# Decoding 64-bit weights in a fused attention and feed-forward kernel: one merge for each part, and earlier second-weight loads

## The chip, the core and the metric

The kernel runs on one core of a Trainium2 chip. A core has five engines that run side by side and wait for each other by semaphores: TensorE (PE, matmuls), VectorE (DVE), ScalarE (ACT), GpSimd (POOL) and SyncE (SP, here only the issuer of DMAs). ScalarE issues some DMAs too. The metric is the device time of one execution in microseconds, from runs on the chip. A profile of one execution gives the rows that are quoted.

## The reference

Causal attention with a forget-gate bias, over 8 batches, 8 heads, 576 tokens and a head size of 64, and behind it a feed-forward block (FFN) from 512 to 2048 and back:

```python
scores = scale * np.matmul(q, k.transpose(0, 1, 3, 2))
s_pos = np.maximum(s, 0.0)
cum = np.cumsum(s_pos, axis=-1)
bias = -(cum[:, :, :, None] - cum[:, :, None, :])
scores = np.where(causal, -1000000000.0, scores + np.minimum(bias, 0.0))
attn = softmax(scores)                      # written out in the original
x = np.matmul(attn, v)                      # heads side by side: 4608 x 512
h = x @ w_in
g = np.where(h >= 1, h, np.where(h <= -1, 0.0, (h + 1) ** 2 / 4))
return (g @ w_out).astype(np.float32)
```

`w_in` (512 x 2048) and `w_out` (2048 x 512) come as 64-bit floats. The kernel gets them as pairs of 32-bit words, `lw` (low) and `hw` (high), and makes 32-bit floats of them on the chip.

## The kernel before

**Attention.** A job is two heads and one half of the query rows (`jobs`, 64 of them). `att_slot(j, k)` takes job `j` in eight slots: operands, six score units, output. A score unit is a matmul into PSUM (`s`, lines 434, 437 and 438), VectorE's reduction with the mask that writes `p` and the row minimum `mn` (line 443), ScalarE's exponential (454), then the scaling by `rs` and the transposes. The first four jobs (`plain`) scale with POOL and ScalarE (474, 472) and transpose on TensorE into `pp` (477, copied at 478); later ones split `p` into two 16-bit parts `pb` and transpose by DMA (508). `att_out` multiplies by `v` into `px`, and `x_split` writes `X`, the FFN's input, under the tag `x0` or `x1`, two buffers each.

**The FFN.** `ffn_h` makes `h` from `X` and `WI` (12 matmuls, line 596), ScalarE and VectorE make `u` (608, 611, 612), ScalarE and POOL split it into `g` (622, 623; tag `g`, four buffers). `ffn_y` multiplies `g` by `WO` (635).

**The weights.** Each weight comes in 16 parts of 128 x 512 numbers (512 KB). `Weights.load` (line 190) takes a raw buffer and issues the DMA on SyncE (line 200). The first weight's raw parts use the four `g` buffers, which the FFN takes over later. The second weight's use `raw`, `x0`, `raw` in turn, two buffers each; `X` of batch 0 also takes an `x0`. Its parts 0 to 2 have `after=w1.r[1]`: a one-column copy (line 195) into the raw buffer, which holds the DMA back until the second row block of the first weight has its scale.

`decode` (line 202) turns a raw part into 32-bit floats: ScalarE writes the absolute value of `hw` read as a float (208); VectorE clamps it from below and takes the peak of each row (209), shifts it by three bits and masks it (210), and puts in sign, exponent bit and the low bits. For even parts (`ACT_LOW`) ScalarE first writes the top bits of `lw` into `hw`'s lower half (215), and one merge follows (216). Odd parts take two merges, sign and exponent (218) and the low bits (219). From the peaks come power-of-two scales: `row_scale` and `row_shares` for the first weight, `scale` for each half of the second (groups of 8 parts), all of them through `exponent` (221). `split` makes two 16-bit parts of each number (257 to 265).

**The order.** The first weight's tasks (`w1_task`, decode part c, load part c + 3, split part c - 4) stand one in three slots among jobs 0 to 3, and the last of them behind these. `w2_tasks` gives the second weight's work: three loads, then for each group eight decodes (each with the load of part c + 3), the scale and eight splits. Six of these tasks come before the main loop, then two for each of its steps, with a higher priority. A planner with its own cost model puts all of it into a fixed order on each engine and each issue queue: it takes by priority whatever it reckons to be ready, so that an instruction without anything to wait for may come long before its place in the program. Each engine then works through its list in that order.

Of the kernel before, what the change touches and what calls it, by code (L numbers as in the profile page):

```python
# [7 lines left out]
BF16 = mybir.dt.bfloat16  # L8
F16 = mybir.dt.float16
F32 = mybir.dt.float32  # L10
F32R = mybir.dt.float32r
I32 = mybir.dt.int32
U16 = mybir.dt.uint16
U8 = mybir.dt.uint8
AF = mybir.ActivationFunctionType
ALU = mybir.AluOpType
# [6 lines left out]
P = 128  # L23
# [10 lines left out]
EPS = 1e-9  # L34
TINY = 2.0 ** -50
LEAST_A = 2.0 ** -5

LEAST_HI = 2.0 ** -15 * 1.125

UNITS = (  # L40
    [(i, hd, 0, QT[i][2]) for i in range(3) for hd in range(2)],
# [10 lines left out]
G_BUFS = 4  # L52
O_BUFS = 3
WO_LAG = 2
# [24 lines left out]
def attention_ffn(ctx: ExitStack, tc: tile.TileContext, qT, kT, vn, s, w_in, w_out, yT):  # L79
    nc = tc.nc  # L80
    LOADQ, CUMQ, FIRSTQ = nc.sync, nc.scalar, nc.sync
    V, A, G, T = nc.vector, nc.scalar, nc.gpsimd, nc.tensor

    cp = ctx.enter_context(tc.tile_pool(name="cp", bufs=1))
    ap = ctx.enter_context(tc.tile_pool(name="ap", bufs=2))
    gp = ctx.enter_context(tc.tile_pool(name="gp", bufs=2))
# [6 lines left out]
    floor_bias = cp.tile([P, 1], F32, name="floor_bias")  # L93
    V.memset(floor_bias, -31.0 / 64.0)

    def pow2floor(out, in_, least):
# [6 lines left out]
        out=ident, in_=ident, pattern=[[-1, P]], compare_op=ALU.not_equal,  # L103
# [13 lines left out]
    def spread(dst, top, name, bank=(ps_s, "s")):  # L117
# [10 lines left out]
        out=mask, in_=mask, pattern=[[-1, S]], compare_op=ALU.is_ge,  # L128
# [40 lines left out]
    NW = 16  # L169
    NC = 512  # L170
    WI = [cp.tile([P, 2, NC], F16, name=f"WI{c}") for c in range(NW)]
    WO = [cp.tile([P, 2, NC], F16, name=f"WO{c}") for c in range(NW + WO_LAG)]

    def flat32(t):
        return t.rearrange("p l n -> p (l n)").bitcast(F32)

    class Weights:
        def __init__(self, name, src, held, out, tags, groups, by_rows=False):
            self.size = NW // (NKT if by_rows else groups)
            self.name, self.src, self.held, self.out, self.tags = name, src, held, out, tags  # L180
            self.peak = cp.tile([P, NW], F32, name=f"peak_{name}")
            self.bound = [cp.tile([P, 1], F32, name=f"bound_{name}{g}") for g in range(groups)]
            self.r = [cp.tile([P, 1], F32, name=f"r_{name}{g}") for g in range(NW // self.size)]
            if by_rows:
                self.rows = cp.tile([P, NKT], F32, name=f"rows_{name}")
                self.shares = cp.tile([P, NKT], F32, name=f"shares_{name}")
            self.raw = {}
            self.act_low, self.pool_lo = ACT_LOW[name], POOL_LO[name]

        def load(self, c, after=None):  # L190
            if c < NW:
                pool, tag, bufs = self.tags[c % len(self.tags)]
                self.raw[c] = pool.tile([P, NC, 2], I32, tag=tag, bufs=bufs, name=f"{self.name}r{c}")
                if after is not None:
                    V.tensor_copy(self.raw[c][:, 0, :1], after.bitcast(I32))
                src = self.src(c)
                dst = self.raw[c]
                if len(src.shape) == 4:
                    dst = dst.rearrange("p (j n) t -> p j n t", j=2)
                nc.sync.dma_start(dst, src)  # L200

        def decode(self, c):
            raw = self.raw.pop(c)
            w = flat32(self.held[c])
            wi = w.bitcast(I32)
            lw, hw = raw[:, :, 0], raw[:, :, 1]

            A.activation(w, hw.bitcast(F32), AF.Abs)
            V.tensor_scalar(w, w, LEAST_HI, LEAST_HI, ALU.max, ALU.max, accum_out=self.peak[:, c:c + 1])
            V.tensor_scalar(wi, wi, 3, 0x3FFFFFF8, ALU.logical_shift_left, ALU.bitwise_and)  # L210

            if c in self.act_low:
                dst = raw.bitcast(U16).rearrange("p n (t f) -> p n t f", f=4)[:, :, 0, 2]
                src = raw.bitcast(U8).rearrange("p n (t f) -> p n t f", f=8)[:, :, 0, 3]
                A.activation(dst, src, AF.Identity, bias=floor_bias, scale=2.0 ** -5)
                V.scalar_tensor_tensor(wi, hw, -0x3FFFFFF9, wi, ALU.bitwise_and, ALU.bitwise_or)
            else:
                V.scalar_tensor_tensor(wi, hw, -0x40000000, wi, ALU.bitwise_and, ALU.bitwise_or)
                V.scalar_tensor_tensor(wi, lw, 29, wi, ALU.logical_shift_right, ALU.bitwise_or)

        def exponent(self, b):
            bi = b.bitcast(I32)
            V.tensor_scalar(bi, bi, 3, -0x40000000, ALU.logical_shift_left, ALU.bitwise_xor)
            V.tensor_scalar(bi, bi, 0x7F800000, None, ALU.bitwise_and)

        def scale(self, g, least):
# [39 lines left out]

    w1 = Weights(
        "wi", lambda c: w_in[c // 4 * P:(c // 4 + 1) * P, c % 4 * NC:(c % 4 + 1) * NC, :],
        WO, WI, ((gp, "g", G_BUFS),), 1, by_rows=True,
    )  # L270
    w2 = Weights(
        "wo", lambda c: w_out[c % 8 * 2 * P:(c % 8 + 1) * 2 * P, c // 8 * NC // 2:(c // 8 + 1) * NC // 2, :]
        .rearrange("(j p) n t -> p j n t", p=P),
        WO[WO_LAG:], WO, ((ap, "raw", 2), (gp, "x0", 2), (ap, "raw", 2)), 2,
    )
    a_in, b_out = w1.bound[0], w2.bound

# [51 lines left out]
    def batch_y(b, groups=(0, 1)):  # L329
        ysc.setdefault(b, {})  # L330
        for i in groups:
            y = ysc[b][i] = ap.tile([P, 1], F32, tag=f"ys{i}", name=f"ys{b}_{i}")
            V.tensor_scalar(y, gsc[b], b_out[i], 2.0 ** -28, ALU.mult, ALU.mult)
# [211 lines left out]
    held = {}  # L545
# [118 lines left out]
        w1.load(c)  # L664
    att_load(0, 0)
    def w2_tasks():
        for c in range(3):
            w2.load(c, w1.r[1])
        for g in range(2):
            for c in range(8 * g, 8 * g + 8):  # L670
                w2.decode(c)
                w2.load(c + 3)
                yield
            w2.scale(g, TINY)
            batch_y(0, (g,))
            for c in range(8 * g, 8 * g + 8):
                w2.split(c)
                yield

    def w1_task(c):  # L680
        w1.decode(c)
        w1.load(c + 3)
        if c >= NKT:
            w1.split(c - NKT)
        if c % NKT == NKT - 1:
            w1.row_scale(c // NKT, LEAST_A)

    c = 0
    for t in range(8 * NPAIR):
        if t % W1_SLOTS == 0:  # L690
            w1_task(c)
            c += 1
        if t == 2:
            load_v(0)
        if t == 6:
            batch_start(0)
        att_slot(t // 8, t % 8)
    for c in range(c, NW):
        w1_task(c)
# [10 lines left out]
    for n, hf in jobs[:NPAIR]:  # L710
        x_split(n, hf, held.pop((n, hf)), shares0)
    tasks = w2_tasks()
    for _ in range(W2_FIRST):
        next(tasks)

    t = 8 * NPAIR
# [56 lines left out]
```

## Time and profile before

| | us |
|---|---|
| median of 3 runs | 1091.19 |
| the runs | 1086.95, 1091.19, 1091.50 |
| the profiled execution | 1091.04 |
| its span, from the first to the last instruction | 1089.2 |

A row of the table of lines has: line, engine, operation, output and inputs, shapes, count; busy time in us and mean ns of one; idle time before them, and what ended it. A row of the answer for one line has the shortest, median and longest duration in ns. A row of a timeline has: start and duration in us, engine (SPq is SyncE's issuing of DMAs), line, operation. A row of waits has: who waited for whom, us in total, times, the longest. In the program's names `wir` and `wor` are the raw parts of the first and the second weight, and `WO` holds either weight's decoded numbers while they wait to be split.

### The profile page before, as it was taken

Reading aid. Unit: us, or ns where it says so; the run is one execution under the profiler, and the core shown is the slowest. Engines: PE = TensorE matmul, PEld = TensorE weight load, DVE = VectorE, ACT = ScalarE, POOL = GpSimd, SP = SyncE. Lnnn points to the kernel's source line nnn. Section 1 sums busy time; section 2 is a strip of 40 time slices with the busy share of each in tenths; the row PEclk is TensorE's granted clock in tenths of the full one; section 3 lists DMA queues with packets and bytes.
Section 4 is the critical chain, followed back from the end, with each engine's and each line's share of the span. In section 5 each row is a group of like instructions: output and inputs, shape, how many; then the busy total and the mean of one; then the engine's idle time right before and its main releaser. Section 6 shows DMA issues by size and latency. Waiting matters only on the chain.

```text
span 1089.2 us, 25029 instructions
## 1 busy us (share of the span) xinstructions
PE 1014.3 (93%) x8494; PEld 778.6 (71%) x8494; DVE 858.7 (79%) x2379; ACT 720.8 (66%) x1707; POOL 658.1 (60%) x1139
## 2 busy tenths in 40 slices
PE   3657889999999999999999999899999999999998
PEld 1334557787778877787778877787778877887787
DVE  7899977678788878887888888788888888887533
ACT  4776675567577675876577765776577765877432
POOL 4643677566577656666567665676577666665522
PEclk9999789999999999999999999999999999999999
DMA  8736543446357773777367753866376662676300
GB/s 248 232 105 191 151 85 82 113 106 160 89 133 151 141 153 74 165 140 163 78 157 140 156 124 88 157 147 157 70 171 142 140 138 69 152 131 140 69 25 20
DMA packets 300839, 140.33 MB, mean 129 GB/s; under 512 B 237608, under 2 KB 286632, under 8 KB 300712
## 3 DMA queue, kind: packets, MB, share of 16 engines
q1 hardware_dynamic: 291008, 128.80, 52.8%
q10 hardware_dynamic: 9704, 9.93, 3.2%
q8 instruction: 67, 1.10, 0.4%
q14 instruction: 60, 0.49, 0.1%
HBM read 71.00 MB, written 9.73 MB: 74 GB/s over the span
## 4 chain that ended last, share of the span: by engine, by line
PE 61%; DVE 10%; ACT 4%; issue 4%; POOL 3%; DMA 1%; ACTq 1%; DVEq 0%; POOLq 0%
PE h L596 26%; PE y L635 25%; PE px L537 4%; PE s L437 3%; PE s L438 3%; DVE pb L507 2%; DVE h L611 1%; DVE p L443 1%; DVE K2s L393 1%; ACT u L608 1%; DVE Q1s L392 1%; DVE u L612 1%; ACT p L454 1%; POOL pb L501 1%; POOL pb L504 1%
## 5 line engine op out<-in xcount | busy, mean ns | idle before, releaser
L596 PE MATMUL h<-x,WI 128*128 128x256 f16 (+1 forms) x3072 | 460.4, 290 | 7.4 <-DVE u L612 4.1
L635 PE MATMUL y<-g,WO 128*128 128x256 f16 (+1 forms) x3072 | 444.0, 286 | 2.0 <-ACT g L622 1.3
L596 PEld LDWEIGHTS <-WI 128*128 128x128 f16 x3072 | 287.8, 99 | 100.5 <-issue 17.7
L635 PEld LDWEIGHTS <-WO 128*128 128x128 f16 x3072 | 286.8, 98 | 83.5 <-issue 4.2
L623 POOL TENSOR_TENSOR g<-u,g 128x320 f16<-128x320 f32 (+1 forms) x256 | 207.3, 810 | 168.9 <-ACT g L622 160.8
L454 ACT ACTIVATE p<-p,mn 64x64 f32<-64x64 f32 (+4 forms) x320 | 179.4, 561 | 108.4 <-DVE mn L443 83.6
L608 ACT ACTIVATE u<-h,ub,us 128x320 f32<-128x320 f32 (+1 forms) x256 | 149.1, 583 | 130.1 <-PE h L596 128.5
L611 DVE SCALAR_TENSOR_TENSOR h<-h,ws,u 128x320 f32<-128x320 f32 (+1 forms) x256 | 132.7, 519 | 91.7 <-ACT u L608 88.5
L501 POOL TENSOR_SCALAR pb<-p,rs 128x256 f16<-128x256 f32 (+4 forms) x148 | 94.7, 640 | 138.6 <-DVE rs L497 86.3
L504 POOL TENSOR_TENSOR pb<-p,pb 128x256 f16<-128x256 f32 (+4 forms) x148 | 157.2, 1062 | 9.9
L443 DVE CUSTOM_DVE_ANT_0 p<-s,mask 64x64 f32<-64x64 f32 (+4 forms) x320 | 134.8, 422 | 29.8 <-PE s L438 19.9
L507 DVE SCALAR_TENSOR_TENSOR pb<-p,rs,pb 128x256 f16<-128x256 f32 (+4 forms) x148 | 128.8, 870 | 23.3 <-POOL pb L501 22.9
L612 DVE SCALAR_TENSOR_TENSOR u<-u,r,h 128x320 f32<-128x320 f32 (+1 forms) x256 | 130.5, 510 | 7.3
L437 PE MATMUL s<-K1s,Q1s 128*128 128x288 f32 (+4 forms) x312 | 118.0, 379 | 10.3 <-DVE mn L443 4.0
L502 ACT ACTIVATE p<-p,rs 128x192 f32<-128x192 f32 (+4 forms) x148 | 84.1, 568 | 48.8 <-DVE rs L497 47.1
L622 ACT CAST g<-u 128x320 f16<-128x320 f32 (+1 forms) x256 | 108.0, 422 | 7.7 <-DVE u L612 6.7
L503 POOL TENSOR_SCALAR pb<-p 128x256 f16<-128x256 f32 (+4 forms) x148 | 88.0, 595 | 21.0 <-ACT p L502 17.0
L438 PE MATMUL s<-K2s,Q2s 68*128 68x288 f32 (+4 forms) x312 | 96.1, 308 | 0.0
L537 PEld LDWEIGHTS <-vt 128*64 128x64 f16 x1464 | 67.5, 111 | 19.1 <-issue 13.6
L537 PE MATMUL px<-pt,vt 128*64 128x256 f16 (+3 forms) x1464 | 77.4, 255 | 1.4 <-DMA pt<-pb 1.3
L437 PEld LDWEIGHTS s<-K1s,Q1s 128*128 128x128 f32 (+1 forms) x312 | 56.5, 181 | 19.7 <-PE s L438 4.5
L393 DVE TENSOR_TENSOR K2s<-rk,K1s 64x1152 fp32r<-64x1152 f32 (+1 forms) x52 | 63.6, 1223 | 6.0 <-ACT K1s L390 4.7
(134 smaller groups left out, 1029.3 us busy)
## 6 DMA issues: line engine op xcount, KB each, us to landing
rk<-in_k_dram SPq DMA_DIRECT2D x56, 288.0 KB
wir<-in_moe_w_in_dram SPq DMA_DIRECT2D x16, 512.0 KB
v<-in_v_dram SPq DMA_DIRECT2D x32, 256.0 KB
wor<-in_moe_w_out_dram SPq DMA_DIRECT2D x16, 512.0 KB
rk<-in_k_dram SPq DMA_DIRECT2D x48, 160.0 KB
rq<-in_q_dram SPq DMA_DIRECT2D x48, 160.0 KB
rq<-in_q_dram SPq DMA_DIRECT2D x56, 128.0 KB
out_dram<-o ACTq DMA_DIRECT2D x32, 160.0 KB
```

The costliest lines, as they stand in the source:

```text
L437: T.matmul(sc[:R, :c1 - c0], Q1[:, hd, qo:qo + R], K1[:, hd, c0:c1], start=True, stop=False)
L443: ttr[0] = V.tensor_tensor_reduce(out=Pt[:R, c0:c1], in0=sc[:R, :c1 - c0], in1=mask[:R, mo:mo + c1 - c0], scale=-0.125, scalar=3.0e38 if m ...
L454: A.activation(Pt[:R, :W], Pt[:R, :W], AF.Exp, bias=m2[:R], scale=-1.0, accum_out=sums[n, i][:R, hd:hd + 1])
L504: G.tensor_tensor(los[1], pw, his[1], ALU.subtract)
L507: V.scalar_tensor_tensor(los[0], pv, rs[:R, :1], his[0], ALU.mult, ALU.subtract)
L537: T.matmul(px[hd * D:(hd + 1) * D, lo:N], vts[n][:, vl, j, hd * D:(hd + 1) * D], PT[:, 4 * j + 2 * hd + pl, lo:], start=(m == 0), stop=(m ...
L596: T.matmul(h[:, :N], WI[4 * kt + ft // 4][:, wl, ft % 4 * P:(ft % 4 + 1) * P], x[:, kt, xl], start=(n == 0), stop=(n == 3 * NKT - 1),)
L608: first = A.activation(u, h[:, :N], AF.Relu, bias=ubi[b], scale=usc[b]).ins
L611: V.scalar_tensor_tensor(h[:, :N], h[:, :N], wsc[b], u, ALU.mult, ALU.max)
L612: V.scalar_tensor_tensor(u, u, r, h[:, :N], ALU.min, ALU.mult)
L623: G.tensor_tensor(g[:, 1], u, g[:, 0], ALU.subtract)
L635: T.matmul(ys[b, hf, m][:, :N], WO[8 * (m // 2) + ft // 2][:, wl, c0:c0 + P], g[:, gl], start=(ft == 0 and n == 0), stop=(ft == NFT - 1 an ...
```

## The change

In `decode`, ScalarE's absolute value is scaled by 2^-112, which brings the exponent into range before the shift; the clamp and the mask go. VectorE shifts (one instruction), and a `tensor_tensor_reduce` adds the two halves of the row and takes the maximum of the sums as the peak. The low bits are put into `hw`'s lower half in both cases: by ScalarE for even parts, by a shift of 16-bit words on VectorE for odd ones. One merge then takes the sign and the low three bits from `hw`. `exponent` loses its shift and exclusive-or, as the peak is now taken from shifted numbers. The raw buffers of the second weight's parts 3 to 6 are the four `g` buffers. Parts 0 to 2 are loaded in the task of the first weight's part 12, with no copy to hold them back, parts 3 to 6 in the tasks of parts 12 to 15, part c + 7 behind the decodes of parts 0 to 2, and part c + 3 from part 7 on.

```diff
-LEAST_HI = 2.0 ** -15 * 1.125
...
+    sums2 = cp.tile([P, NC // 2], BF16, name="sums2")
...
             if c < NW:
-                pool, tag, bufs = self.tags[c % len(self.tags)]
+                pool, tag, bufs = self.tag(c)
...
-            lw, hw = raw[:, :, 0], raw[:, :, 1]
-
-            A.activation(w, hw.bitcast(F32), AF.Abs)
-            V.tensor_scalar(w, w, LEAST_HI, LEAST_HI, ALU.max, ALU.max, accum_out=self.peak[:, c:c + 1])
-            V.tensor_scalar(wi, wi, 3, 0x3FFFFFF8, ALU.logical_shift_left, ALU.bitwise_and)
-
+            hw = raw[:, :, 1]
+
+            A.activation(w, hw.bitcast(F32), AF.Abs, scale=2.0 ** -112)
+            V.tensor_scalar(wi, wi, 3, None, ALU.logical_shift_left)
+            half = w.shape[1] // 2
+            V.tensor_tensor_reduce(
+                out=sums2, in0=w[:, :half], in1=w[:, half:], scale=1.0, scalar=0.0,
+                op0=ALU.add, op1=ALU.max, accum_out=self.peak[:, c:c + 1],
+            )
+
+            low = raw.bitcast(U16).rearrange("p n (t f) -> p n t f", f=4)[:, :, 0, 2]
             if c in self.act_low:
-                dst = raw.bitcast(U16).rearrange("p n (t f) -> p n t f", f=4)[:, :, 0, 2]
                 src = raw.bitcast(U8).rearrange("p n (t f) -> p n t f", f=8)[:, :, 0, 3]
-                A.activation(dst, src, AF.Identity, bias=floor_bias, scale=2.0 ** -5)
-                V.scalar_tensor_tensor(wi, hw, -0x3FFFFFF9, wi, ALU.bitwise_and, ALU.bitwise_or)
+                A.activation(low, src, AF.Identity, bias=floor_bias, scale=2.0 ** -5)
             else:
-                V.scalar_tensor_tensor(wi, hw, -0x40000000, wi, ALU.bitwise_and, ALU.bitwise_or)
-                V.scalar_tensor_tensor(wi, lw, 29, wi, ALU.logical_shift_right, ALU.bitwise_or)
+                src = raw.bitcast(U16).rearrange("p n (t f) -> p n t f", f=4)[:, :, 0, 1]
+                V.tensor_scalar(low, src, 13, None, ALU.logical_shift_right)
+            V.scalar_tensor_tensor(wi, hw, -0x7FFFFFF9, wi, ALU.bitwise_and, ALU.bitwise_or)

         def exponent(self, b):
             bi = b.bitcast(I32)
-            V.tensor_scalar(bi, bi, 3, -0x40000000, ALU.logical_shift_left, ALU.bitwise_xor)
             V.tensor_scalar(bi, bi, 0x7F800000, None, ALU.bitwise_and)
...
-        WO[WO_LAG:], WO, ((ap, "raw", 2), (gp, "x0", 2), (ap, "raw", 2)), 2,
+        WO[WO_LAG:], WO,
+        lambda c: (gp, "g", G_BUFS) if 3 <= c < 7
+        else ((ap, "raw", 2), (gp, "x0", 2), (ap, "raw", 2))[(c if c < 3 else c + 2) % 3], 2,
...
     def w2_tasks():
-        for c in range(3):
-            w2.load(c, w1.r[1])
         for g in range(2):
             for c in range(8 * g, 8 * g + 8):
                 w2.decode(c)
-                w2.load(c + 3)
+                if c < 3:
+                    w2.load(c + 7)
+                elif c >= 7:
+                    w2.load(c + 3)
                 yield
...
     def w1_task(c):
         w1.decode(c)
         w1.load(c + 3)
+        if c == NW - 4:
+            for d in range(3):
+                w2.load(d)
+        if c >= NW - 4:
+            w2.load(c - NW + 7)
```

More of the change, by code (lines that the diff above doesn't have):

```diff
@@ L177, in attention_ffn, with __init__ @@
     class Weights:
-        def __init__(self, name, src, held, out, tags, groups, by_rows=False):
+        def __init__(self, name, src, held, out, tag, groups, by_rows=False):
             self.size = NW // (NKT if by_rows else groups)
-            self.name, self.src, self.held, self.out, self.tags = name, src, held, out, tags
+            self.name, self.src, self.held, self.out, self.tag = name, src, held, out, tag
             self.peak = cp.tile([P, NW], F32, name=f"peak_{name}")
@@ L268, in attention_ffn @@
         "wi", lambda c: w_in[c // 4 * P:(c // 4 + 1) * P, c % 4 * NC:(c % 4 + 1) * NC, :],
-        WO, WI, ((gp, "g", G_BUFS),), 1, by_rows=True,
+        WO, WI, lambda c: (gp, "g", G_BUFS), 1, by_rows=True,
     )
```

## The prediction

> **What bounds the kernel now.** I read the page first, then the windows by stage, then what TensorE waited for, then the decode's rows, then the timelines of SyncE and VectorE. The columns of a window are the busy time of PE, PEld, DVE, ACT and POOL (each with its instructions), the granted clock, the DMA share and GB/s.
>
> ```profile
> span 1089.2 us, 25029 instructions
> PE 1014.3 (93%) x8494; PEld 778.6 (71%) x8494; DVE 858.7 (79%) x2379; ACT 720.8 (66%) x1707; POOL 658.1 (60%) x1139
> ```
> ```profile
> 0.00:20.00 20.00, 3.31 (x10) 1.73 (x10) 14.49 (x37) 7.62 (x14) 7.30 (x22) 1.00 0.82 242
> 20.00:120.00 100.00, 66.98 (x215) 37.01 (x216) 91.21 (x277) 73.44 (x161) 53.26 (x80) 0.95 0.62 184
> 120.00:150.00 30.00, 26.23 (x171) 16.10 (x170) 24.35 (x69) 17.90 (x37) 16.46 (x20) 0.82 0.59 123
> 150.00:1089.20 939.20, 917.82 (x8103) 723.72 (x8101) 728.62 (x1999) 621.80 (x1498) 581.11 (x1018) 1.00 0.55 121
> ```
>
> TensorE is idle for 1089.2 - 1014.3 = 74.9 us. After 150 us it is busy 917.8 of 939.2: the matmuls set the time there, and nothing of the change lies there. Before 150 us it is idle 16.7 + 33.0 + 3.8 = 53.5 us. That start is where the weights are decoded, so the question is how much of those 53.5 us goes. From 20 to 120 us VectorE is busy 91.2 of 100 us, TensorE 67, and TensorE's longest waits are:
>
> ```profile
> PE s L434 <- DVE mn L443: 13.6, 9, 5.1
> PE pp L477 <- POOL p L474: 11.1, 4, 5.1
> PE col_wi L122 <- DVE t_wi L120: 3.1, 1, 3.1
> ```
>
> Two of the three end with VectorE, 16.7 us; the POOL step in between needs VectorE's `rs` as well. So in this stage **VectorE is the bound**, through an order fixed in advance, in which score reductions, weight decoding and scale chains queue behind one another.
>
> **The change, part by part: the decode.** Its groups in the table of lines, all on VectorE (busy us, mean ns):
>
> ```profile
> L209 DVE TENSOR_SCALAR_CACHE_REDUCE WO<-WO 128x512 f32<-128x512 f32 x32 | 21.6, 678 | 7.9 <-ACT WO L208 7.8
> L210 DVE TENSOR_SCALAR WO<-WO 128x512 int32<-128x512 int32 x32 | 17.2, 537 | 0.1
> L216 DVE SCALAR_TENSOR_TENSOR WO<-wir,WO 128x512 int32<-128x512 int32 x8 | 7.1, 884 | 0.0
> L218 DVE SCALAR_TENSOR_TENSOR WO<-wir,WO 128x512 int32<-128x512 int32 x8 | 6.4, 798 | 0.0
> L219 DVE SCALAR_TENSOR_TENSOR WO<-wir,WO 128x512 int32<-128x512 int32 x8 | 6.1, 766 | 0.0
> L218 DVE SCALAR_TENSOR_TENSOR WO<-wor,WO 128x512 int32<-128x512 int32 x8 | 6.1, 759 | 0.0
> L219 DVE SCALAR_TENSOR_TENSOR WO<-wor,WO 128x512 int32<-128x512 int32 x8 | 6.0, 754 | 0.0
> L216 DVE SCALAR_TENSOR_TENSOR WO<-wor,WO 128x512 int32<-128x512 int32 x8 | 5.9, 741 | 0.0
> L209 DVE DVE_READ_ACCUMULATOR WO<-WO 128x1 f32 x32 | 2.5, 79 | 0.0
> ```
> ```profile
> L209 DVE TENSOR_SCALAR_CACHE_REDUCE WO<-WO x32: 664/678/687, 6.9 to 144.3; 128x512 f32<-128x512 f32 x32
> L210 DVE TENSOR_SCALAR WO<-WO x32: 394/416/1619, 8.1 to 145.1; 128x512 int32<-128x512 int32 x32
> L216 DVE SCALAR_TENSOR_TENSOR WO<-wir,WO x8: 672/683/1877, 9.4 to 65.4; 128x512 int32<-128x512 int32 x8
> L443 DVE CUSTOM_DVE_ANT_0 p<-s,mask 128x320 f32<-128x320 f32 x64 | 30.9, 484 | 6.9 <-PE s L438 5.5 <-PE s L434 0.5
> L443 DVE CUSTOM_DVE_ANT_0 p<-s,mask 128x192 f32<-128x192 f32 x64 | 22.3, 349 | 6.7 <-PE s L438 2.9 <-PE pp L477 2.0 <-PE s L434 1.2
> ```
>
> Before: 21.6 + 2.5 + 17.2 + 13.0 (L216) + 12.5 (L218) + 12.1 (L219) = 78.9 us for 32 parts. After, for each part:
> - the shift stays one instruction of L210's form: 17.2 us in all;
> - the clamp gives way to `tensor_tensor_reduce` over 256 columns, the instruction of L443. Halfway between 192 columns (349 ns) and 320 (484) is 417 ns. But L443 reads PSUM and the mask, while the new one reads two SBUF halves, as the merges do, and those are stretched now and then: the 48 of L216, L218 and L219 take 37.6 us, 783 ns each, against a median of 683, so 0.10 more. I take 0.52 x 32 = 16.6 us, and 2.5 for the accumulator reads. Bounds: 0.42 without the stretch, 0.78 if it goes no faster than L209 over 512 columns and is stretched as well;
> - ScalarE's step on even parts stays. Odd parts get a shift of 512 strided 16-bit elements, which the trace doesn't show. Its nearest row is L210, the same operation on as many elements: 0.537 x 16 = 8.6 us. Bounds: L210's median 0.416, and a merge's 0.783;
> - one merge for each part: 32 x 0.783 = 25.1 us.
>
> The sum is 17.2 + 16.6 + 2.5 + 8.6 + 25.1 = 70.0 us, a saving of 8.9. The exponent's removed instruction and the three gate copies come on top, 6 x 0.14 + 3 x 0.14 = 1.2:
>
> ```profile
> L223 DVE TENSOR_SCALAR rows_wi<-rows_wi x4: 138/141/147, 22.8 to 70.9; 128x1 int32<-128x1 int32 x4
> L195 DVE COPY wor<-r_wi x3: 134/141/143, 47.7 to 87.6; 128x1 int32<-128x1 int32 x3
> ```
>
> That is **10.1 us of VectorE work less**. With both good ends it is 78.9 - (17.2 + 13.4 + 2.5 + 6.7 + 25.1) + 1.2 = 15.2; with both bad ends 78.9 - (17.2 + 25.0 + 2.5 + 12.5 + 25.1) + 1.2 = -2.2. ScalarE's `Abs` with a scale is taken at its old price, as nothing is added to its elements.
>
> The stretch in this sum is what a rule speaks of. L209 never leaves 664 to 687 ns; L216 reaches 1877. The Trainium skill, "SBUF — State Buffer", section "Who interferes with whom", says that a VectorE instruction with two SBUF inputs contends with GpSimd's reads, and that the accumulating `tensor_scalar` does not. The trace agrees: the clamp that goes was immune, its replacement isn't. Without this rule the saving would be 3.2 us larger, by it what I took.
>
> How much of the 10.1 us lies on the path? Only three of the 32 peaks are taken after 120 us:
>
> ```profile
> 120.44 0.67 DVE L209 TENSOR_SCALAR_CACHE_REDUCE WO<-WO 128x512 f32<-128x512 f32 x1
> ...
> 134.53 0.69 DVE L209 TENSOR_SCALAR_CACHE_REDUCE WO<-WO 128x512 f32<-128x512 f32 x1 [0.49 <-ACT WO L208]
> ...
> 144.28 0.69 DVE L209 TENSOR_SCALAR_CACHE_REDUCE WO<-WO 128x512 f32<-128x512 f32 x1 [3.45 <-ACT WO L208]
> ```
>
> So 29/32 falls in the stage that VectorE bounds, at 91% busy: 10.1 x 29/32 x 0.91 = **8.3 us** (with the bounds -1.8 to 12.5). What is late next is POOL's and ScalarE's part of the first four jobs.
>
> **The loads.** Rows of the issue queue, then of VectorE, ScalarE and TensorE:
>
> ```profile
> 18.85 2.62 SPq L365 DMA_DIRECT2D rq<-in_q_dram  x2
> ...
> 27.58 4.10 SPq L200 DMA_DIRECT2D wir<-in_moe_w_in_dram  x4
> ...
> 47.87 1.29 SPq L200 DMA_DIRECT2D wor<-in_moe_w_out_dram  x2
> ...
> 129.87 0.40 SPq L200 DMA_DIRECT2D wor<-in_moe_w_out_dram  x1
> ...
> 137.34 0.38 SPq L200 DMA_DIRECT2D wor<-in_moe_w_out_dram  x1
> ```
> ```profile
> 40.79 0.68 DVE L219 SCALAR_TENSOR_TENSOR WO<-wir,WO 128x512 int32<-128x512 int32 x1
> ...
> 87.65 0.14 DVE L195 COPY wor<-r_wi 128x1 int32<-128x1 int32 x1
> ```
> ```profile
> 32.25 0.66 ACT L208 ACTIVATE WO<-wir 128x512 f32<-128x512 f32 x1
> ```
> ```profile
> 20.00:30.00 10.00, 6.87 (x19) 4.00 (x19) 9.46 (x39) 7.92 (x22) 5.14 (x9) 1.00 0.97 256
> ```
> ```profile
> 147.70 0.44 PE L635 MATMUL y<-g,WO 128*128 128x320 f16 x2
> ```
> ```profile
> 86.80 0.69 DVE L216 SCALAR_TENSOR_TENSOR WO<-wor,WO 128x512 int32<-128x512 int32 x1
> ```
> ```profile
> 109.72 0.44 ACT L622 CAST g<-u 128x320 f16<-128x320 f32 x1
> ```
>
> Before, parts 0 and 2 come at 47.87; part 1 sits behind its gate copy until 87.65, because `X` for batch 0 takes an `x0` buffer first. Parts 1, 4, 7, 10 and 13 then share one buffer, load after decode after load: the issues at 129.87 and 137.34 are the last two links, and they hold the first `y` matmul back to 147.70. After the change part 1 has its buffer before `X`, parts 3 to 6 have four buffers of their own, and the chain is 1, 8, 11, 14. Group 0 is then ready to decode when VectorE has time for it. What this brings TensorE is at most its 3.8 idle us between 120 and 150; I take half, 1.9, as no row says that all of it waits for these parts.
>
> The price: the gate is gone. `rq` at 18.85 belongs to job 12 (`F32_JOBS`), issued eleven jobs early as soon as the queue had nothing nearer to do. Parts 0 to 2 are as free and come earlier in the program, so I expect them **ahead of `rq`, not behind the last first-weight part**, and ahead of first-weight parts 7 to 10 at 27.58. The DMA share there is 0.97 at 256 GB/s: 3 x 524 KB are 6.1 us, paid once. Part 7 is read at 32.25 and finished at 40.79 + 0.68; its decode needs about 2 us of VectorE, so 6.5 us of delay fit. Only part 1 is new work before 60 us: 2.0 us, which I charge in full. SyncE's own seven issues are 0.4 us each and nobody's wait. The first FFN tiles `g` must wait for parts 3 to 6 to be decoded; part 6 has its merge at 86.80 already now, 23 us ahead of the first `g` at 109.72, so this costs 0, and if part 3 were late, at most one decode, 2 us.
>
> The sum: -8.3 - 1.9 + 2.0 = -8.2. The profiled execution took 1091.04 us (span 1089.2 and 1.8 around it), the median of three is 1091.19, so the same base: **1091.0 - 8.2 = 1082.8 us**. Within 0.5%, 5.5 us, is about what a measurement of this kernel can't tell from no change.
>
> **The rivals.**
> - A, the path of the first jobs: what VectorE saves it then waits, because scores, exponentials, POOL's scaling and the transposes of jobs 0 to 3 set the start. For: POOL's 11.1 us; VectorE itself waits for `pp` there. Against: 91% busy. Then only the 29/32 of the 16.7 us share of 33.0 counts, 10.1 x 29/32 x 0.51 = 4.6, less the 2.0 of part 1: 1088.4.
> - B, slower: **the ungated parts crowd the first weight's loads.** 6.1 us against 6.5 of room is close. If parts 7 to 10 land later than VectorE can use them, the delay passes on to 11 to 15 through their four buffers, the first weight's half of the saving is waited away, and decodes of second-weight parts 0 to 2 (3 x 2.2 us) stand ahead of it: 6.1 + 6.6 - 8.3 / 2 = +8.5, 1099.5; without the displaced decodes 1093. It decides from a delay of 6.5 us at part 7. Against: DMA is at 0.62 on average from 20 to 120.
> - C, more: filled gaps also bring the clock back. It is 0.95 over 67.0 busy us and 0.82 over 26.2, a loss of 3.3 + 4.7 = 8.0 us. If `y` work stands ready from some 125 us and TensorE no longer pauses, that goes too: 1074.8. The Trainium skill, "TensorE: Matmul & The Clock Gate", Part 1, says that the clock halves after an idle window of about 3.4 us. Here the granted clock falls in the stretch with TensorE's later waits but was 1.00 in the emptier first 20 us, so the trace bears this out in part.
>
> **How the numbers follow.** Forecast 0.50, A 0.24, B 0.12, C 0.14. The forecast's own spread is 1078.5 to 1089 by the unit prices; a tenth of its chance lies within 0.5%. Range: 1074 to 1093, which takes in the bounds -1.8 and 12.5, A and C, and leaves out most of B. Faster by over 0.5%: 0.45 + 0.14 + 0.02 of A = 0.61; within: 0.05 + 0.22 + 0.02 = 0.29; slower: 0.10.
>
> **What would show it.** Right: the reduction near 0.5 us and the strided shift near 0.5; VectorE's busy total down by about 10 us; second-weight loads 0 to 2 at some 19 us; the first `y` before 130 us; TensorE's idle before 150 us at about 45; the stretch from 150 on unchanged. Wrong: the reduction at 0.7 or more; part 7's `Abs` after 39 us; VectorE with new idle time between 30 and 70 us; or an order after 150 us in which TensorE's idle time changes by several us, which no row here foretells.

## The result, and the profile after

| | before | after |
|---|---|---|
| median, us (20 runs each) | 1091.97 | 1085.29 |
| lowest to highest | 1086.95 to 1095.71 | 1082.76 to 1089.84 |
| ratio after / before, 95% interval | | 0.9946 [0.9932, 0.9959] |
| profiled execution, us | 1091.04 | 1084.4 |

The change makes the kernel 0.54% faster, with an interval that lies clear of no change. The forecast was 1082.8, the range 1074 to 1093. In the changed file decode's lines are 208 (absolute value), 209 (32-bit shift), 211 (halves), 222 (strided 16-bit shift) and 223 (merge); the score reduction is 448, POOL's scaling 479, `h` 601, `y` 640.

The head of the page after, then its windows by stage (columns as before):

```profile
span 1082.6 us, 24990 instructions
PE 1010.8 (93%) x8494; PEld 775.7 (72%) x8494; DVE 851.4 (79%) x2370; ACT 722.7 (67%) x1707; POOL 665.9 (62%) x1139
```
```profile
20.00:120.00 100.00, 67.61 (x232) 36.65 (x234) 90.55 (x289) 77.68 (x168) 63.05 (x83) 0.95 0.72 199
120.00:150.00 30.00, 27.25 (x213) 18.67 (x210) 26.15 (x66) 24.10 (x47) 23.03 (x27) 0.99 0.32 79
150.00:1082.60 932.60, 912.63 (x8044) 718.71 (x8042) 721.18 (x1983) 612.68 (x1481) 572.33 (x1010) 1.00 0.55 122
```

The span is 6.6 us shorter: TensorE's idle time falls from 74.9 to 1082.6 - 1010.8 = 71.8, which gives 3.1, and its busy time falls by 3.5 for the same 8494 matmuls. By 150 us it has begun 8494 - 8044 = 450 of them; before it was 391. From 20 to 120 us, where I had looked for the gain, VectorE is as busy as before (90.55 us against 91.21) and TensorE has gained 0.6 us.

The `h` matmuls from 120 to 150 us, first in the answer for that line, then in its windows (before, then after), show the other half:

```profile
L596 PE MATMUL h<-x,WI x82: 297/299/475, 119.7 to 145.8; 128*128 128x320 f16 x82
```
```profile
120.00:150.00 30.00, 14.85 (x82) 8.70 (x80) 0.82 0.59 123
```
```profile
L601 PE MATMUL h<-x,WI x96: 297/299/310, 121.9 to 148.9; 128*128 128x320 f16 x96
```
```profile
120.00:150.00 30.00, 14.36 (x96) 9.20 (x96) 0.99 0.32 79
```

Before, some of them take 475 ns in place of 299, and the 82 cost 14.85 / 82 = 181 ns of TensorE each; after, none is over 310 and they cost 150. At 150 the old 82 would have taken 2.6 us less. The clock there went from 0.82 to 0.99.

The decode's groups after:

```profile
L209 DVE TENSOR_SCALAR WO<-WO 128x512 int32<-128x512 int32 x32 | 18.6, 580 | 5.0 <-ACT WO L208 5.0
L211 DVE CUSTOM_DVE_ANT_0 sums<-WO 128x256 bf16<-128x256 f32 x32 | 17.0, 531 | 0.0
L223 DVE SCALAR_TENSOR_TENSOR WO<-wir,WO 128x512 int32<-128x512 int32 x16 | 12.9, 814 | 1.6 <-ACT wir L219 1.5
L223 DVE SCALAR_TENSOR_TENSOR WO<-wor,WO 128x512 int32<-128x512 int32 x16 | 12.7, 806 | 0.0
L222 DVE TENSOR_SCALAR wor<-wor 128x512 uint16<-128x512 uint16 x8 | 7.8, 979 | 0.0
L222 DVE TENSOR_SCALAR wir<-wir 128x512 uint16<-128x512 uint16 x8 | 6.8, 853 | 0.0
```

With 2.5 us of accumulator reads they sum to 78.3 us, against 78.9 before and 70.0 forecast. The halves came as worked out (531 ns against 520). The strided shift did not: 14.6 us for 8.6, a mean of 915 ns, outside its bound of 783. Records of neighbours overlap on this engine (in VectorE's timeline below a merge begins at 79.74 and lasts 0.67, to 80.41, and its neighbour begins at 80.34), so both sums are somewhat high; but both decodes have four instructions for an even part and five for an odd one, so their difference stands: by these rows the new decode saves VectorE 0.6 us and not 8.9. VectorE's busy total, in which overlaps count once, fell by 858.7 - 851.4 = 7.3 us, where about 10 was forecast. How much of that is the decode's, the experiments tell.

SyncE's timeline after, and the rows of the `h` and `y` lines (first start behind the durations):

```profile
18.95 5.12 SPq L200 DMA_DIRECT2D wor<-in_moe_w_out_dram  x3
24.11 0.60 SPq L370 DMA_DIRECT2D rq<-in_q_dram  x1
```
```profile
L601 PE MATMUL h<-x,WI x3072: 269/298/471, 94.3 to 1074.3; 128*128 128x320 f16 x96, 128*128 128x256 f16 x96
L640 PE MATMUL y<-g,WO x3072: 269/296/471, 112.3 to 1078.2; 128*128 128x320 f16 x96, 128*128 128x256 f16 x96
```

Parts 0 to 2 are issued at 19 us, ahead of `rq`, as foreseen. The first `y` comes at 112.3 and not at 147.7; the first `h` hardly moves (95.6 to 94.3). What TensorE waits for from 20 to 120 us after:

```profile
PE pp L482 <- POOL p L479: 14.8, 7, 7.4
PE s L439 <- DVE mn L448: 10.8, 9, 2.7
```

The wait for POOL's scaling has grown from 11.1 to 14.8 us, with one wait of 7.4. That is new, and POOL's own timeline has it:

```profile
78.47 5.82 POOL L479 TENSOR_SCALAR p<-p,rs 128x192 f32<-128x192 f32 x1 [2.84 <-DVE rs L474]
87.23 0.54 POOL L479 TENSOR_SCALAR p<-p,rs 128x320 f32<-128x320 f32 x1 [1.49 <-DVE rs L474]
```
```profile
77.20 0.68 DVE L223 SCALAR_TENSOR_TENSOR WO<-wor,WO 128x512 int32<-128x512 int32 x1
...
78.42 1.39 DVE L268 SCALAR_TENSOR_TENSOR WI<-WO,r_wi,WI 128x512 f16<-128x512 f32 x2
79.74 0.67 DVE L223 SCALAR_TENSOR_TENSOR WO<-wor,WO 128x512 int32<-128x512 int32 x1
80.34 0.41 DVE L211 CUSTOM_DVE_ANT_0 sums<-WO 128x256 bf16<-128x256 f32 x1
...
80.75 1.39 DVE L268 SCALAR_TENSOR_TENSOR WI<-WO,r_wi,WI 128x512 f16<-128x512 f32 x2
```

A scaling of 192 columns takes 5.82 us here, when one of 320 takes 0.54 nine us later; before the change the longest of these twelve was 1.234 us:

```profile
L474 POOL TENSOR_SCALAR p<-p,rs x12: 310/636/1234, 19.6 to 84.4; 64x64 f32<-64x64 f32 x4, 128x192 f32<-128x192 f32 x4, 128x320 f32<-128x320 f32 x4
```

VectorE, in the timeline behind POOL's, works through decodes of the second weight and splits of the first in one piece from 77 to 84 us. The Trainium skill, "SBUF — State Buffer", section "Who interferes with whom", says that a VectorE instruction with two SBUF inputs contends with a GpSimd instruction that reads SBUF. The trace agrees in so far as VectorE's merges, halves and splits run back to back until 83.99 us and the scaling ends at 84.29. The decodes of this piece stand between the last row scale of the first weight (76.5 us) and the shares that the first `h` needs: from the row scale to `shares0` it takes 15.1 us, to 91.6, and before it was 13.7 (73.2 to 86.9).

### The profile page after: what moved, and what is told of

Same layout as the page of the kernel before. It is cut to its first block, busy times and chain, and to the rows that moved or that the text cites. A ratio compares the mean times of both kernels' runs of the same rounds, so it can differ in the third digit from the quotient of the medians.

```text
span 1082.6 us, 24990 instructions
## 1 busy us (share of the span) xinstructions
PE 1010.8 (93%) x8494; PEld 775.7 (72%) x8494; DVE 851.4 (79%) x2370; ACT 722.7 (67%) x1707; POOL 665.9 (62%) x1139
## 4 chain that ended last, share of the span: by engine, by line
PE 66%; DVE 14%; ACT 7%; DMA 5%; issue 4%; POOL 2%; ACTq 1%; SPq 1%; DVEq 0%; POOLq 0%
PE h L601 27%; PE y L640 27%; PE px L542 4%; PE s L442 3%; PE s L443 3%; DVE pb L512 2%; DVE p L448 2%; PE s L439 2%; DVE h L616 2%; ACT u L613 1%; ACT p L459 1%; DVE K2s L398 1%; DMA v<-in_v_dram 1%; DMA wir<-in_moe_w_in_dram 1%; ACT o L654 1%
## 5 line engine op out<-in xcount | busy, mean ns | idle before, releaser
L459 ACT ACTIVATE p<-p,mn 64x64 f32<-64x64 f32 (+4 forms) x320 | 179.6, 561 | 107.2 <-DVE mn L448 82.3
L508 POOL TENSOR_SCALAR pb<-p 128x256 f16<-128x256 f32 (+4 forms) x148 | 89.1, 602 | 19.6 <-ACT p L507 14.6
L542 PEld LDWEIGHTS <-vt 128*64 128x64 f16 x1464 | 67.3, 111 | 19.7 <-issue 14.6
```

The source lines that it names most:

```text
L459: A.activation(Pt[:R, :W], Pt[:R, :W], AF.Exp, bias=m2[:R], scale=-1.0, accum_out=sums[n, i][:R, hd:hd + 1])
L542: T.matmul(px[hd * D:(hd + 1) * D, lo:N], vts[n][:, vl, j, hd * D:(hd + 1) * D], PT[:, 4 * j + 2 * hd + pl, lo:], start=(m == 0), stop=(m ...
```

## The experiments

Two theories stood at first. **The work:** VectorE's saved decode time sets the gain. **The loads:** what matters is when the second weight's parts come. Within the second there were three candidates: the gate that is gone, the four `g` buffers, and what the early parts push back. Each expectation says what these would give. Ratios are to the kernel before on the same chip, with 95% intervals.

**The decode alone** (the kernel before with the new `decode` and `exponent`, loads untouched):

```diff
...
-            V.tensor_scalar(w, w, LEAST_HI, LEAST_HI, ALU.max, ALU.max, accum_out=self.peak[:, c:c + 1])
-            V.tensor_scalar(wi, wi, 3, 0x3FFFFFF8, ALU.logical_shift_left, ALU.bitwise_and)
+            V.tensor_scalar(wi, wi, 3, None, ALU.logical_shift_left)
+            V.tensor_tensor_reduce(
...
```

> The kernel before with the new decode and exponent alone; loads, their gate copies and buffers as before. Theory V (VectorE's shorter decode brings the gain, as the prediction had it): 4 to 7 us faster than before, ratio 0.994 to 0.996, first y matmul some 6 us earlier than 147.7. Theory L (the earlier loads bring it, by undoing the chain of parts 1, 4, 7, 10 and 13 on one buffer): within 1.5 us of before, ratio 0.9985 to 1.0015, first y matmul still after 140 us.

Measured: 1091.19 us, 0.9993 [0.9971, 1.0016]. No gain. The head of its page, two of its windows, its halves, and what ScalarE waited for from 20 to 120 us:

```profile
PE 1019.4 (93%) x8494; PEld 778.6 (71%) x8494; DVE 856.9 (78%) x2373; ACT 722.9 (66%) x1707; POOL 657.1 (60%) x1139
```
```profile
20.00:120.00 100.00, 67.88 (x211) 36.09 (x212) 82.28 (x258) 68.71 (x153) 53.25 (x81) 0.93 0.62 167
120.00:150.00 30.00, 27.74 (x163) 16.69 (x162) 28.93 (x74) 23.42 (x44) 15.26 (x17) 0.79 0.64 167
```
```profile
L211 DVE CUSTOM_DVE_ANT_0 sums<-WO 128x256 bf16<-128x256 f32 x32 | 21.3, 665 | 0.1
```
```profile
ACT WO L208 <- DMA wor<-in_moe_w_out_dram: 9.6, 5, 2.8
ACT WO L208 <- DMA wir<-in_moe_w_in_dram: 8.8, 6, 2.5
```

VectorE is busy 82.3 us from 20 to 120 us, not 91.2. But from 120 to 150 it is busy 28.9 us, not 24.4, and over the whole span its total falls only by 858.7 - 856.9 = 1.8 us: most of that work came later, it did not go away. The halves take 665 ns on average here, and the decode's rows sum to 80.0 us, against 78.9 before. The decode's first step waits 18.4 us for raw parts, against 8.8 + 2.1 = 10.9 before, which fits with the decodes coming later. So this run shows that the new decode alone brings no time; it took hardly any work off VectorE, so it can't show what a real saving there would be worth.

**The loads alone** (the kernel after with the old decode):

```diff
...
-            V.tensor_scalar(wi, wi, 3, None, ALU.logical_shift_left)
-            V.tensor_tensor_reduce(
...
+            V.tensor_scalar(w, w, LEAST_HI, LEAST_HI, ALU.max, ALU.max, accum_out=self.peak[:, c:c + 1])
+            V.tensor_scalar(wi, wi, 3, 0x3FFFFFF8, ALU.logical_shift_left, ALU.bitwise_and)
...
```

> The changed kernel with the old decode and exponent; loads and buffers as changed. V: within 1.5 us of before. L: 5 to 7 us faster than before, ratio 0.9935 to 0.9955, first y matmul before 120 us as in the changed kernel (112.3).

Measured: 1087.82, 0.9963 [0.9943, 0.9984]. So the loads alone bring some two thirds of the gain, though this interval and that of the whole change overlap. VectorE's busy total is 852.8 us in this kernel, with the old decode: 5.9 of the 7.3 us came with the loads, and the new decode adds 852.8 - 851.4 = 1.4. On these loads it is worth 0.9963 - 0.9946 = 0.17%, on the old ones 0.07%, and neither is clear of nothing; 0.07 and 0.37 add up to the whole 0.54 within the noise.

**The gate put back** into the kernel after:

```diff
-                w2.load(d)
+                w2.load(d, w1.r[1])
```

> The changed kernel with the gate back on second-weight parts 0 to 2 (a copy of the first weight's second row scale into the raw buffer ahead of each load), in the same place of the program, so that part 1 still has its buffer ahead of X. Crowding theory: the three ungated loads at 18.95 us cost the first weight's loads 2 us or more, so this is 2 to 4 us faster than the changed kernel (1081 to 1083 against 1085.3). No crowding: within 1.5 us of the changed kernel, as DMA has room again by the time it matters.

Measured: 1092.84, 1.0020 [0.9999, 1.0040]: the whole gain is gone, which neither theory had. SyncE's timeline of this kernel:

```profile
43.36 3.60 SPq L200 DMA_DIRECT2D wir<-in_moe_w_in_dram  x2
47.05 1.41 SPq L200 DMA_DIRECT2D wor<-in_moe_w_out_dram  x3
```

Parts 0 to 2 go out at 47 and no longer at 19 us, and the first `h` starts at 100.7. The rival that the ungated parts make the kernel slower by crowding the first weight's loads falls here: taking them out of its way costs 8 us by the ratios, and gains nothing.

**No `g` buffers** (the kernel after, parts 0 to 2 still ungated and ahead of `X`, but `raw`, `x0`, `raw` in turn and part c + 3 behind each decode, as before):

```diff
-        lambda c: (gp, "g", G_BUFS) if 3 <= c < 7
-        else ((ap, "raw", 2), (gp, "x0", 2), (ap, "raw", 2))[(c if c < 3 else c + 2) % 3], 2,
+        lambda c: ((ap, "raw", 2), (gp, "x0", 2), (ap, "raw", 2))[c % 3], 2,
...
-                if c < 3:
-                    w2.load(c + 7)
-                elif c >= 7:
-                    w2.load(c + 3)
+                w2.load(c + 3)
...
-        if c >= NW - 4:
-            w2.load(c - NW + 7)
```

> The changed kernel with the second weight's parts in raw, x0, raw in turn as before and part c + 3 loaded behind each decode; parts 0 to 2 still ungated and ahead of X. If it is part 1's place ahead of X that undoes the chain: within 1.5 us of the changed kernel. If the four g buffers for parts 3 to 6 are needed: at least half of the gain is lost, 1088 us or more, and the first y matmul comes after 125 us, as parts 4, 7, 10 and 13 still follow part 1 on one buffer.

Measured: 1080.90, 0.9903 [0.9875, 0.9931], the best so far, and outside what either theory gave. So three early parts are enough; having seven in flight, with the `g` buffers and the earlier issue that goes with them, costs about 0.4% (0.9946 against 0.9903). The `h` line of this kernel, and the answer for POOL's scaling:

```profile
L600 PE MATMUL h<-x,WI x3072: 269/292/474, 88.7 to 1072.0; 128*128 128x320 f16 x96, 128*128 128x256 f16 x96
```
```profile
L478 POOL TENSOR_SCALAR p<-p,rs x12: 312/642/1297, 20.1 to 83.8; 64x64 f32<-64x64 f32 x4, 128x192 f32<-128x192 f32 x4, 128x320 f32<-128x320 f32 x4
```

The first `h` comes 5.6 us earlier than in the kernel after, no scaling is held beyond 1.3 us, and from the row scale to `shares0` it is 7.4 us (74.5 to 81.9): most of the decodes that stood in between come later.

**The same with the old decode**, to price the decode where the loads are early:

```diff
...
-                V.tensor_scalar(low, src, 13, None, ALU.logical_shift_right)
-            V.scalar_tensor_tensor(wi, hw, -0x7FFFFFF9, wi, ALU.bitwise_and, ALU.bitwise_or)
+                V.scalar_tensor_tensor(wi, hw, -0x40000000, wi, ALU.bitwise_and, ALU.bitwise_or)
+                V.scalar_tensor_tensor(wi, lw, 29, wi, ALU.logical_shift_right, ALU.bitwise_or)
...
```

> e4 with the old decode and exponent: what the new decode is worth once the raw parts are there in time. Interaction theory (the decode's saving counts only where VectorE is not waiting for parts; e1 gave 0.8 us): 4 to 6 us slower than e4, 1085 to 1087. If the decode is worth nothing anywhere: within 1.5 us of e4, 1079.5 to 1082.5.

Measured: 1089.34, 0.9957 [0.9940, 0.9974]. Against 0.9903 with the new decode that is 0.54%, or 5.9 us, give or take 0.33% (two chips, each against its own runs of before). With the gated loads the same decode was worth 0.07%, with the change's loads 0.17%. VectorE's busy total falls by 859.0 - 852.4 = 6.6 us here, where it fell by 1.8 and 1.4 us there, though by the decode's own rows it is only 78.7 - 77.2 = 1.5. So the decode pays most in the order in which VectorE's total falls most. That this is because its parts are there in time fits, but is not shown.

**POOL's scaling on ScalarE** in the kernel after, for the first four jobs:

```diff
-            if hd:
-                A.activation(Pt[:R, :W], Pt[:R, :W], AF.Copy, scale=rs[:R, 1:])
-            else:
-                G.tensor_scalar(Pt[:R, :W], Pt[:R, :W], rs[:R, :1], 1.0, ALU.mult, ALU.mult)
+            A.activation(Pt[:R, :W], Pt[:R, :W], AF.Copy, scale=rs[:R, hd:hd + 1])
```

> The changed kernel with the scaling of the first four jobs (the POOL instruction that TensorE waits for 14.8 us between 20 and 120 us, against 11.1 before) moved to ScalarE. If POOL, stretched by VectorE's instructions with two SBUF inputs, holds back the start: 3 to 6 us faster than the changed kernel. If TensorE's waits there are only the last link behind VectorE: within 1.5 us of it.

Measured: 1087.89, 0.9950 [0.9932, 0.9968], the same as the change's 0.9946. With POOL out of that chain, and ScalarE doing its work, the time is what it was: nothing shows that the 5.82 us scaling, striking as it is, holds the kernel.

**The decodes from part 3 on held** on VectorE until `shares0` is written, in the kernel after:

```diff
+                with tc.issue_after(ready) if c >= 3 else ExitStack():
-                w2.decode(c)
+                    w2.decode(c)
...
-        V.tensor_scalar(shares0, w1.shares, rcs[0], None, ALU.mult)
+        ready = V.tensor_scalar(shares0, w1.shares, rcs[0], None, ALU.mult).ins
```

> The changed kernel with VectorE's instructions of the decodes of second-weight parts 3 to 15 placed behind the one that makes shares0; loads and the four g buffers as changed. Theory G (the seven early parts give the planner second-weight decodes to put between the first weight's last row scale and shares0, 15.3 us apart in the changed kernel against 7.5 in e4, and so hold back x and the first h): the stretch falls to 8 us or less, the first h comes 5 us earlier (89), and the time falls to e4's level, 1079 to 1082. Rival S (the four g buffers cost by themselves, through SyncE's queue or the FFN's g waiting for them): within 1.5 us of the changed kernel, 1084 to 1087.

Measured: 1085.52, 0.9931 [0.9907, 0.9955]. The stretch shrinks as foreseen (72.5 to 80.8, 8.3 us) and the first `h` comes at 88.4, but the time moves little, and lies in the range of rival S: only part of the theory holds. TensorE's idle time from 50 to 95 us fell from 45.0 - 29.0 = 16.0 to 10.2 us, and yet the span was 1084.9.

**All decodes of the second weight held**, parts 0 to 2 too:

```diff
+                with tc.issue_after(ready) if True else ExitStack():
-                w2.decode(c)
+                    w2.decode(c)
...
```

> As e6, but parts 0 to 2 are held behind shares0 too. If decoding parts 0 to 2 at 35 to 55 us fills time in which VectorE waits for the first weight's DMAs: 3 to 5 us slower than e6 (three decodes of about 1.7 us move into the full stretch). If that time was not idle: within 1.5 us of e6.

Measured: 1088.32, 0.9957 [0.9935, 0.9978], 2.8 us above the kernel just told, on the same chip. The intervals overlap, and that kernel, measured once more below, comes to 0.9951. So it is not shown that decoding parts 0 to 2 at 35 to 55 us is some of what the missing gate brings.

**Prices by themselves**, in a small program with VectorE's forms in turn:

```diff
...
+        return V.tensor_scalar(r4[:, :, 0, 2], r4[:, :, 0, 1], 13, None, ALU.logical_shift_right)
...
+        return V.tensor_scalar(lone[:, :, 1], lone[:, :, 0], 13, None, ALU.logical_shift_right)
...
+        return G.tensor_scalar(pin, pin, 1.0, 1.0, ALU.mult, ALU.mult)
...
```

> Left out: everything but VectorE instructions of the decode's forms, eight of each by themselves, then eight of each beside a GpSimd scaling of 1024 numbers for every second one; the output is zeros. Theory (the strided 16-bit shift is dear by itself): alone it takes 0.70 to 0.75 us for 512 elements, the contiguous 32-bit shift 0.42, the strided 32-bit shift about 0.42; the halves' sum 0.40 to 0.42 alone and over 0.5 in the mean beside GpSimd, the clamp 0.66 in both phases. Rival (the 0.73 in the kernel is contention with GpSimd, or an overlap in the records): alone the strided 16-bit shift takes 0.42 to 0.54, no more than the 32-bit one, and grows only in the second phase.

The planner put all of GpSimd's scalings beside the first round, and the second round ran alone. Its groups (L36 is the strided 16-bit shift, L40 the contiguous one, L43 the strided 32-bit shift, L50 the halves):

```profile
L36 DVE TENSOR_SCALAR lone<-lone 128x512 uint16<-128x512 uint16 x8 | 5.9, 734 | 0.3
...
L43 DVE TENSOR_SCALAR lone<-lone 128x512 int32<-128x512 int32 x8 | 3.4, 428 | 0.3
L50 DVE CUSTOM_DVE_ANT_0 sums<-w 128x256 bf16<-128x256 f32 x8 | 3.4, 424 | 0.3
L40 DVE TENSOR_SCALAR lone<-lone 128x512 uint16<-128x512 uint16 x8 | 2.3, 294 | 0.3
```

The strided 16-bit shift is dear by itself: 734 ns against 428 for the same step over 32-bit words. It is the 16-bit stride, not contention, that my nearest row (L210, 32-bit) did not have. Beside GpSimd it gets worse. The timeline of the first round:

```profile
15.48 6.26 POOL L60 TENSOR_SCALAR pin<-pin 128x1024 f32<-128x1024 f32 x5
16.02 1.45 DVE L36 TENSOR_SCALAR lone<-lone 128x512 uint16<-128x512 uint16 x1
17.51 4.38 DVE L40 TENSOR_SCALAR lone<-lone 128x512 uint16<-128x512 uint16 x4
```

The same shift takes 1.45 us, and four contiguous ones 4.38, or 1.1 each where alone they took 0.294. The halves, the clamp and the merge did not meet GpSimd in this program, so the halves' stretch beside it is not shown here.

**The kernel after, and two variants, once more**, all on one chip:

> The kernel after, once more, beside the two variants on one chip. Theory (half-clock matmuls account for the rest between the variants and belong to the program's order): ratio 0.9946 within 0.0015, and this execution again has under 0.5 us of h and y excess over 0.3 us between 120 and 150 us, some 8.5 us in all. Rival (the clock falls by chance in each execution): the excess moves by 3 us or more from the first profile of the same program.

> The kernel without the four g buffers, once more. Theory: ratio 0.990 within 0.002, 4 us below the kernel after on this chip; excess of h and y matmuls over 0.3 us again about 8.3 us in all and none from 120 to 150. Rival (chance): the excess moves by 3 us or more, and the two kernels' intervals overlap widely.

> The kernel after with the decodes from part 3 on held behind the scaled shares, once more. Theory: ratio 0.993 within 0.002; the excess of h and y matmuls is again some 4 to 5 us above that of the kernel without g buffers (13.0 against 8.3 us), as large as the difference of their spans. Rival (chance): the excess is within 2 us of the other's or below it, while the time stays behind by 3 us; then the difference lies elsewhere.

| | median, us | lowest to highest | ratio | profiled span, first and now |
|---|---|---|---|---|
| after | 1085.13 | 1084.15 to 1087.96 | 0.9942 [0.9920, 0.9964] | 1082.6, 1082.7 |
| no `g` buffers | 1079.44 | 1079.00 to 1082.71 | 0.9889 [0.9852, 0.9925] | 1080.3, 1080.9 |
| decodes from part 3 held | 1087.34 | 1082.49 to 1089.94 | 0.9951 [0.9927, 0.9975] | 1084.9, 1080.7 |

The three times are as before; holding the decodes brings nothing that can be told. Its two profiled spans differ by 4.2 us for one program in one order. The windows of its `h` matmuls, first execution and second:

```profile
120.00:150.00 30.00, 12.14 (x72) 7.52 (x72) 0.92 0.30 69
150.00:200.00 50.00, 15.03 (x96) 9.84 (x96) 0.93 0.45 103
```
```profile
120.00:150.00 30.00, 10.75 (x72) 7.03 (x72) 0.97 0.29 74
150.00:200.00 50.00, 15.90 (x116) 11.09 (x117) 1.00 0.47 104
```

An `h` matmul cost (12.14 + 15.03) / 168 = 162 ns and then (10.75 + 15.90) / 188 = 142: over 168 that is 3.3 us of the 4.2. The second profile is of the fastest of its twelve runs. In all, what `h` and `y` matmuls last beyond 0.3 us each comes to 13.5 and then 9.0 us here, to 9.5 and 9.3 in the kernel after, to 9.2 and 10.9 without `g` buffers: only the first moved by as much as the rival asked for. Before 120 us the half clock stays with the program: the same line's window from 90 to 120 us shows a granted clock of 0.69 in both of these executions, of 0.84 and 0.83 in the two of the kernel after. So the theory that the half clock belongs to a program's order holds there; behind 120 us it falls, and chance, its rival, holds. The Trainium skill, "TensorE: Matmul & The Clock Gate", Part 1, says that the window which decides on the clock runs freely and does not start with the kernel, so that the same kernel meets it differently from run to run; these two executions agree with that behind 120 us. The kernel after, too, had no slow `h` between 120 and 150 us in its first profile, and in the second its 96 took 15.43 us, not 14.36. The better order (no `g` buffers) keeps its lead of 5.7 us over the kernel after on one chip, and its slowest run (1082.71) lies below the other's fastest (1084.15), so that lead is not this chance.

## Why the prediction was right, and where it was not

- **The decode's saving**, "10.1 us of VectorE work less", was the step that failed; the forecast put -8.3 us on it. In its place: the rows of the decode sum to 78.3 us for 78.9, and on the loads as before or as changed the new decode takes only 1.8 or 1.4 us off VectorE's total. The decode alone takes 0.07% off the time, with an upper end of 0.29% or 3 us. Of the 8.3 us between the forecast's 70.0 and 78.3, the strided shift has 6.0: it was mis-sized, 915 ns on average for 537, as a 32-bit row stood for a 16-bit stride. The 32-bit shift's group also grew, 17.2 to 18.6 us. Halves (531 ns for 520) and merges (810 for 783) came as worked out in the kernel after, but the halves took 665 in the decode-only kernel. The rule of the Trainium skill, "SBUF — State Buffer", section "Who interferes with whom", was rightly used: the halves reach 1.375 us, where the clamp never left 664 to 687 ns.
- **The bound.** "VectorE is the bound" from 20 to 120 us stays open: the decode did not take its 10 us of work off VectorE. The one pair in which VectorE's total falls much with the decode (6.6 us, without `g` buffers) has a time 5.9 us lower, which fits with a bound. A busy share of 91% could not show it. It said that VectorE had work, not that the work came first: the loads alone gain 0.37% with VectorE at 91.7 us in the same stage.
- **The loads.** -1.9 + 2.0 was near nothing; measured are 0.37% by themselves, and 0.74% between the kernel after (0.9946) and the same with the gate (1.0020), some 8 us. The order was foreseen (ahead of `rq`, at 19 us, first `y` before 130), the worth was not: I counted the three ungated parts as a price for the DMA queues, and they are the part of the change that pays. What I had credited instead, the four `g` buffers, costs 0.4% with the load order that goes with it.
- **Rival B** (crowding): wrong in the time. The first steps of first-weight parts 7 to 10 do come later, at 34.4 to 47.0 us for 32.3 to 38.3, but the decode alone, with its loads as before, has them at 33.5 to 43.9. A DMA share of 0.97 was no limit in bytes: between 20 and 30 us it was 256 GB/s, and 337 after the change at 1.01.
- **Rival A**, saved work that then waits on the path of jobs 0 to 3, had no saving of the size to work with, so no run decides on it. What grew in the decode-only kernel were ScalarE's waits for raw parts, 10.9 to 18.4 us.
- **Rival C** (the clock): partly right, though not as a gain to count on. 2.6 us of `h` time between 120 and 150 us came back in the profiled pair, most of the 3.5 us by which TensorE's busy time fell; in a second profile of the kernel after 1.1 us of that was gone again. Its other term, 3.3 us from the clock of 0.95 before 120 us, rests on a figure that leaves out the time before 100.1 us, and so does "was 1.00 in the emptier first 20 us": the trace has no clock records there, and TensorE ran at about half speed (last section). So the row that stood against the clock rule says nothing against it.
- **TensorE's idle time** before 150 us was to be 45; it is 16.7 + 32.4 + 2.8 = 51.9, against 53.5. After 150 us it was to stay: 21.4 before, 20.0 after.

So the forecast of a gain and the range held, and 1082.8 stood 2.5 us from 1085.3, but that was luck: two errors offset each other, a gain put on the decode that its instructions don't bring, and a worth of the early loads that was taken for a cost. Through which chain the earlier parts bring their time is not shown step by step. Why holding the late decodes shortens the wait for the first `h` by six us and saves no time is not settled; its longer half-clock stretch between 90 and 120 us (0.69 for 0.84) may be part of it. That the early decodes between row scale and `shares0` are what the `g` buffers cost is therefore argued, not shown; that those buffers, with their load order, cost it is shown.

## What to carry to other kernels

An engine that is busy for 91% of a stage has work; that alone does not make it the bound. Before a saving on it is credited, check that there is one: sum the rows of the old and the new instructions, and look at the engine's total over the whole span, since a window can lose 8.9 us of work that only moves out of it. Then price the edits singly and together; the same decode was worth 0.07, 0.17 and 0.54% in three orders, and only the last is clear of nothing. Open the earliest gate first and price added buffers by themselves: deeper prefetch hands a planner work that it may put in front of the chain that matters. An operation on strided 16-bit words needs a row of its own, as a 32-bit one is no stand-in.

## What the hardware showed that was not expected

**TensorE ran at about half speed for its first 93 us, and the granted clock of a window does not show it.** Three windows of the kernel after, each with fp32 score matmuls of one shape and, where there are any, f16 `h` matmuls (the third figure from the end of a window's row is the granted clock):

```profile
86.00:92.00 6.00, 6.00 (x14) 3.12 (x13) 5.56 (x22) 3.09 (x10) 0.84 (x3) 1.00 0.00 0
L439 PE MATMUL s<-K1w,Q1w 68*128 68x288 f32 x4 | 2.4, 712 | 0.0
```
```profile
95.00:98.00 3.00, 3.00 (x22) 2.07 (x20) 2.07 (x7) 2.35 (x4) 3.00 (x5) 1.00 0.67 196
L601 PE MATMUL h<-x,WI 128*128 128x320 f16 x18 | 2.7, 299 | 0.0
L439 PE MATMUL s<-K1w,Q1w 68*128 68x288 f32 x2 | 0.6, 404 | 0.0
```
```profile
103.40:110.30 6.90, 6.37 (x22) 3.40 (x22) 6.64 (x18) 4.83 (x9) 4.26 (x4) 0.51 0.70 240
L601 PE MATMUL h<-x,WI 128*128 128x320 f16 x19 | 5.2, 465 | 0.3 <-DVE u L617 0.3
L439 PE MATMUL s<-K2w,Q2w 68*128 68x288 f32 x2 | 1.3, 767 | 0.3 <-DVE mn L448 0.3
```

The last two windows show what the clock does: at 0.51 an `h` takes 465 ns and a score of 288 columns 767, at 1.00 they take 299 and 404. The rule on the clock's halving from the same part of the Trainium skill, "TensorE: Matmul & The Clock Gate", Part 1, draws no line between the types, and neither do these rows. But from 86 to 92 us, also at 1.00, the score takes 712 ns. The clock records of this trace begin at 93.2 us, and a stretch without a record counts as 1.00. The kernel without `g` buffers bears this out: its first profile has records from 46.2 us on, the window from 50 to 90 us shows 0.50, and its scores of 192 columns take 567 ns there, as long as the 568 of the kernel after at a shown 1.00. The mean clock of a run has the same gap: the two executions of that kernel have 0.973 and 0.990, and spans of 1080.3 and 1080.9 us.

So a granted clock of 1.00 should be held against the time of one matmul shape before it is believed. In the kernel before, the records begin at 100.1 us, and TensorE is busy 55.6 us until then; by the ratio of 404 to 712 ns an estimate is that some 24 us of that are the slow clock. It is also a rival that no run here separates from the order of the weights: the long slow stretch of the start ends at 100.1 us before, 93.2 after, 90.5 without `g` buffers and 104.7 with the gate back, in the order of their times; but with the decode alone it ends at 91.6, and that kernel gains nothing.
